# The opening of an attention block: halved loads from two queues, and a narrower first score tile

## The chip, the cores and the metric

The kernel runs on one core of one Trainium2 chip. The metric is the device time of one execution in microseconds (us), the median over several runs. The program keeps five engines busy: TensorE (PE; its weight loads are shown apart as PEld), VectorE (DVE), ScalarE (ACT), GpSimd (POOL) and SyncE (SP, which here only issues transfers). Each engine takes its instructions in order, and waits on semaphores for the others.

## What is computed

```python
q_bits = (einsum('bhsd,dk->bhsk', q, proj) > 0)
k_bits = (einsum('bhsd,dk->bhsk', k, proj) > 0)
mask = (bucket(q_bits)[..., :, None] == bucket(k_bits)[..., None, :])
scores = where(mask, q @ k.T / sqrt(64), -1e9)
x = softmax(scores) @ v            # 2 batches, 8 heads, 768 rows, 64 columns
x = gate(conv(x)) * (x @ w_val) @ w_out
u = x + real(fft2(x)); out = u + relu(norm(u) @ w_ch1) @ w_ch2
```

Queries and keys are hashed by six projections into buckets; a query attends to keys of its own bucket alone. Only the hashing and the first scores are touched here.

## The kernel before

**The stages.** `attention` walks eight pairs of heads, two heads (j = 0, 1) to a pair and six tiles of 128 query rows to a head: 96 score tiles, numbered n. Behind it come the gated projection, the Fourier mixing and a stage of channel weights. The order of the instructions is the order in which the Python code emits them (a manual schedule); nothing is reordered later.

**One score tile.** `scores(n)` multiplies a query tile by all 768 keys in two passes m (line 557). Row group m = 0 of the tiles `q2` and `k2` holds the high part of q and k, doubled; m = 1 holds in its upper half the low part of k and the high part of q, and in its first seven rows the hash bits, so that one product gives the score and pushes unequal buckets far away. `clamp(n)` on DVE (line 568) takes the minimum, `expo(n)` on ACT (line 575) the exponential, `p_transpose` turns it on PE (line 593), `p_high` on ACT and `p_low` on DVE split it, and `pv` multiplies by v (line 616). The loop over n clamps tile n+3 while it turns tile n.

**Where q and k come from.** `load(p, j)` (line 326) lets SP issue q and k of one head as one transfer each. PE turns them (64 columns of q and 64 of k beside each other, so that q lands on partitions 0 to 63 and k on 64 to 127), ACT writes the high part `ht`, DVE the low part `lt`. For the first head `start()` copies them into `q2[0]` and `k2[0]` by ACT and POOL. For the second head `qk_place(0, 1)` (lines 411 to 416) lets SP issue six transfers into `q2[1]` and `k2[1]`, and `bits_place` (line 435) two more for the bits. `scores(6)`, the first tile of the second head, waits for all eight.

**The bits of the first head.** `proj` is loaded into the tile `pr`; `project_parts(j)` splits it on POOL (lines 174, 377, 379 and 382) into `ph`, `pl` and `plus`; `project_alone` (line 448) multiplies on PE into the PSUM tile `whole`; DVE compares with zero (lines 504 and 509); for k a second step on ACT (line 505) scales the bits into `k2[0]`. The table `col` holds scale and bias by partition.

**Warm-up.** `idle(n)` (line 356) issues n matmuls of zeros: 18 ahead of the first data, three and four later.

Of the kernel before, what the change touches and what calls it, by code (L numbers as in the profile page):

```python
# [34 lines left out]
WARM = (18, 3, 4)  # L35
# [48 lines left out]
def col_table():  # L84

    c = np.zeros((P, 6), np.float32)
    c[:64, 0] = 1.0
    c[64:, 0] = KSCALE
    c[:, 2] = -1.0
    c[0, 2] = 1.0  # L90
    c[:, 3] = -8.0 * 896 * 2.0 ** 20
    c[:, 4] = -8.0 * 897 * 2.0 ** 20

    for j in (0, NR):
        c[j : j + NB, 1] = 1.0
        c[j : j + NB, 5] = -0.5
        c[j + NB, 5] = 1.0
        c[j + 32 : j + 32 + NB, 1] = -2.0 * BIG
        c[j + 32 : j + 32 + NB, 5] = BIG
        c[j + 32 + NB, 5] = 3.0 * BIG  # L100
    return c
# [3 lines left out]
def block_kernel(  # L105
# [15 lines left out]
    warm = cpool.tile([P, 1], F32, name="warm")  # L121
    nc.vector.memset(warm, 0.0)

# [178 lines left out]
    def attention(es):  # L302
# [24 lines left out]

        def load_v(p):
# [41 lines left out]
        def project_parts(j):  # L370

            for half in range(2):
# [3 lines left out]
                pool_copy(hd, pr[rs, :])  # L376
                nc.gpsimd.tensor_tensor(ld, f32(hd), pr[rs, :], op=ALU.subtract)
                pool_copy(pl[rs, j, c0 : c0 + NB], f32(hd))
                nc.gpsimd.tensor_tensor(plus[rs, j, c0 : c0 + NB], pr[rs, :], f32(hd), op=ALU.subtract)
# [12 lines left out]
        def qk_transpose(p, j, a):  # L392
# [11 lines left out]
            nc.scalar.activation(ht, tp, AF.Copy, scale=col[:, 0:1])  # L404
            nc.vector.scalar_tensor_tensor(lt, tp, col[:, 0:1], f32(ht), op0=ALU.mult, op1=ALU.subtract)
# [54 lines left out]
        def start():  # L460
# [7 lines left out]
            def turned(j, tps):  # L468
                for a in range(2):
                    for r in range(3):  # L470
                        nc.tensor.transpose(
                            tps[a][:, r * P : (r + 1) * P], rqk[:, j, 3 * a + r].rearrange("p i d -> p (i d)"), ident
                        )

            def high(j, tps):
                for a in range(2):
                    nc.scalar.activation(halves(st[0]["ht", j])[a], tps[a], AF.Copy, scale=col[:, 0:1])

            def low(j, tps):
# [950 lines left out]
```

## Time and profile before

| what | value |
| --- | --- |
| median of three runs | 617.75 us (617.74, 617.75, 620.0) |
| span of the profiled execution (first to last instruction) | 616.8 us |
| PE busy | 604.7 us, 98% |
| DVE, ACT, POOL busy | 444.7, 358.5, 269.3 us |
| first score matmul that waits for bits starts | 10.75 us into the span |
| first clamp starts | 11.40 us |

The profiled execution has no time of its own beside the three that are listed; its span is 0.95 us below their median, and that difference is taken to be what lies around the span. A busy share is an average over the stages, and the opening is 2% of the span: what it costs is read from its own rows, and what it is worth later from the stage into which it runs.

### The profile page before, as it was taken

Reading aid. Unit: us, or ns where it says so; the run is one execution under the profiler, and the core shown is the slowest. Engines: PE = TensorE matmul, PEld = TensorE weight load, DVE = VectorE, ACT = ScalarE, POOL = GpSimd, SP = SyncE. Lnnn points to the kernel's source line nnn. Section 1 sums busy time; section 2 is a strip of 40 time slices with the busy share of each in tenths; the row PEclk is TensorE's granted clock in tenths of the full one; section 3 lists DMA queues with packets and bytes.
Section 4 is the critical chain, followed back from the end, with each engine's and each line's share of the span. In section 5 each row is a group of like instructions: output and inputs, shape, how many; then the busy total and the mean of one; then the engine's idle time right before and its main releaser. Section 6 shows DMA issues by size and latency. Waiting matters only on the chain.

```text
span 616.8 us, 10435 instructions
## 1 busy us (share of the span) xinstructions
PE 604.7 (98%) x3711; PEld 537.4 (87%) x3711; DVE 444.7 (72%) x850; ACT 358.5 (58%) x712; POOL 269.3 (44%) x303
## 2 busy tenths in 40 slices
PE   7999999999999999999999999999999999999997
PEld 6889999999998889998898988888888888888886
DVE  5999999999999998898669788888885411111113
ACT  5998899998998887944625355555665111111121
POOL 8152588876888799892350633233221000000000
PEclk9999999999999999999999999999999999999999
DMA  6956686756666640262110243443440200000002
GB/s 139 210 142 164 145 178 160 164 152 156 157 154 178 171 124 14 73 231 70 36 35 0 70 133 118 125 136 108 134 135 1 103 0 1 2 0 1 0 1 102
DMA packets 54957, 62.02 MB, mean 101 GB/s; under 512 B 29184, under 2 KB 42664, under 8 KB 54650
## 3 DMA queue, kind: packets, MB, share of 16 engines
q1 hardware_dynamic: 54170, 57.81, 35.7%
q0 software_dynamic: 432, 3.55, 1.5%
q8 instruction: 29, 0.48, 0.3%
q14 instruction: 22, 0.18, 0.1%
q10 hardware_dynamic: 304, 0.01, 0.0%
HBM read 36.73 MB, written 3.19 MB: 65 GB/s over the span
## 4 chain that ended last, share of the span: by engine, by line
PE 78%; DVE 10%; DMA 4%; ACT 2%; issue 2%; SPq 2%; POOL 1%; DVEq 0%; ACTq 0%; POOLq 0%
PE pf L1337 20%; PE acc L1347 20%; PE sp L557 8%; PE op L616 7%; PE ptp L593 6%; PE ps L1154 5%; PE ps L222 3%; PE ps L1218 3%; DVE sd L568 2%; DVE ptl L605 2%; PE ps L1189 1%; DMA rqk<-in_k_dram 1%; PE late L222 1%; DMA xs<-xc 1%; PE bp L443 1%
## 5 line engine op out<-in xcount | busy, mean ns | idle before, releaser
L1347 PE MATMUL acc<-w,hid 128*128 128x512 f32 x576 | 137.4, 391 | 0.0
L1347 PEld LDWEIGHTS acc<-w,hid 128*128 128x128 f32 x576 | 105.5, 188 | 20.1
L1340 DVE SCALAR_TENSOR_TENSOR hid<-pf,hid 128x512 fp32r<-128x512 f32 (+1 forms) x62 | 33.4, 555 | 120.6 <-ACT hid L1339 120.6
L1337 PE MATMUL pf<-uth,w 128*128 128x512 f32 (+1 forms) x496 | 97.1, 337 | 0.1
L568 DVE TENSOR_SCALAR_CACHE_REDUCE sd<-sp 128x768 f32<-128x768 f32 x96 | 91.1, 950 | 7.7 <-PE sp L557 7.2
L1339 ACT ACTIVATE hid<-pf 128x512 fp32r<-128x512 f32 (+1 forms) x62 | 28.9, 488 | 115.2 <-PE pf L1337 115.2
L557 PE MATMUL sp<-qk 128*128 128x512 f32 (+1 forms) x384 | 91.5, 360 | 3.9 <-DVE sd L568 2.6
L605 DVE TENSOR_TENSOR ptl<-ptp,pth 128x768 fp32r<-128x768 f32 x96 | 91.4, 952 | 5.1 <-ACT pth L601 3.8
L1337 PEld LDWEIGHTS pf<-uth,w 128*128 128x128 f32 x496 | 79.0, 188 | 15.2 <-DVE hid L1340 1.3
L575 ACT ACTIVATE sd<-sd,nm 128x768 f32<-128x768 f32 x96 | 90.1, 939 | 1.5 <-DVE sd L568 1.5
L601 ACT CAST pth<-ptp 128x768 fp32r<-128x768 f32 x96 | 77.0, 802 | 17.7 <-PE ptp L693 8.9
L162 POOL TENSOR_TENSOR w<-cv 128x512 fp32r<-128x512 f32 x31 | 40.1, 1293 | 88.8 <-DVE cv L157 77.4
L593 PE MATMUL ptp<-ident,sd 128*128 128x128 f32 x576 | 78.6, 272 | 0.2 <-ACT sd L575 0.2
L616 PE MATMUL op<-pth,v 128*128 128x256 f32 x288 | 74.0, 283 | 1.0 <-ACT xc L629 1.0
L616 PE MATMUL op<-ptl,v 128*128 128x256 f32 x288 | 73.8, 286 | 0.0
L557 PEld LDWEIGHTS sp<-qk 128*128 128x128 f32 x384 | 58.2, 189 | 13.6 <-DVE sd L568 7.1
L593 PEld LDWEIGHTS ptp<-ident,sd 128*128 128x128 f32 x576 | 65.8, 140 | 1.1 <-ACT sd L575 0.5
L634 POOL TENSOR_TENSOR xm<-xc,xs 64x256 f32<-64x256 f32 x48 | 35.2, 734 | 59.2 <-DMA xs<-xc 38.6
L616 PEld LDWEIGHTS op<-pth,v 128*128 128x128 f32 x288 | 54.2, 188 | 5.9 <-ACT xc L629 2.0
L616 PEld LDWEIGHTS op<-ptl,v 128*128 128x128 f32 x288 | 54.3, 188 | 0.3
L1337 PE MATMUL pf<-utl,w 128*128 128x512 f32 (+1 forms) x248 | 53.1, 336 | 0.0
L149 ACT ACTIVATE cv<-cv,col 128x512 int32<-128x512 int32 x32 | 23.2, 725 | 41.5 <-DVE cv L146 41.5
(214 smaller groups left out, 998.0 us busy)
## 6 DMA issues: line engine op xcount, KB each, us to landing
raw<-in_moe_w_ch_dram SPq DMA_DIRECT2D x32, 512.0 KB
qk<-ht SPq DMA_DIRECT2D x60, 192.0 KB
qk<-lt SPq DMA_DIRECT2D x30, 192.0 KB
rqk<-in_q_dram SPq DMA_DIRECT2D x16, 192.0 KB
rqk<-in_k_dram SPq DMA_DIRECT2D x16, 192.0 KB
rv<-in_v_dram SPq DMA_DIRECT2D x8, 384.0 KB
out_dram<-o SPq DMA_DIRECT2D x12, 256.0 KB
xs<-xc SPq DMA_DIRECT2D x47, 64.0 KB
```

The costliest lines, as they stand in the source:

```text
L162: nc.gpsimd.tensor_tensor(dst()[1], fold(g.bitcast(F32)), fold(e.bitcast(F32)), op=ALU.mult)
L557: nc.tensor.matmul(sp[:, cs], q2[i][:, m, qi * P : (qi + 1) * P], k2[i][:, m, cs], start=m == order[0], stop=m == order[1])
L568: nc.vector.tensor_scalar(sd[n], sp, CLAMP, None, op0=ALU.min, op1=ALU.min, accum_out=st[p]["nm"][:, n % 12 : n % 12 + 1],)
L575: nc.scalar.activation(sd[n], sd[n], AF.Exp, bias=st[p]["nm"][:, i : i + 1], scale=-1.0, accum_out=st[p]["sums"][:, i : i + 1],)
L593: nc.tensor.transpose(tp[:, r // 3, c0 : c0 + P], sd[n][:, r * P : (r + 1) * P], ident)
L601: nc.scalar.copy(p_parts(n)[0], tp)
L605: nc.vector.tensor_tensor(lo, tp, f32(ho), op=ALU.subtract)
L616: nc.tensor.matmul(po[kb], v3[:, r, c0 : c0 + P], pt[kb][x][:, r, :], start=r == 0 and x == 0, stop=r == R - 1 and x == 1,)
L634: add[kb] = lambda: nc.gpsimd.tensor_tensor(st[p]["xm"][mr, blk * QB : (blk + 1) * QB], xc[mr, :], xs[mr, :], op=ALU.add)
L1337: nc.tensor.matmul(pf, w[:, c, :], x[:, c, cs], start=n == 0, stop=n == 3 * NC - 1)
L1340: nc.vector.scalar_tensor_tensor(hl[:, cs], pf, 0.0, f32(hh)[:, cs], op0=ALU.max, op1=ALU.subtract)
L1347: nc.tensor.matmul(acc, x[:, ts_], w, start=f == 0 and n == 0, stop=f == NF - 1 and n == 2)
```

## The change

Five things change in the first 12 us of the program.

1. `load_halves` replaces the first `load(0, 0)`: q and k of the first head come in two halves each, q issued by SP and k by ACT. `proj` follows on both queues, one half from each. 13 instead of 18 warm-up matmuls stand ahead.
2. `project_parts(0)` and the sign of `pr` run on DVE instead of POOL, ahead of the first low parts. The scale of the turned tiles comes from a constant written by DVE, no longer from `col`.
3. k's bits are written by DVE straight into `k2[0]`; q's bits are compared on DVE and then scaled on ACT, in pieces of 128, 256 and 384 columns. So the two roles are exchanged, with the columns of `col`.
4. Of q only the first 128 columns are copied ahead; the other 640 come in three POOL copies. k's first copy on POOL is split in two.
5. The second head is turned into two other PSUM banks; its two high and two low parts are spread between the first clamps and exponentials.

```diff
-WARM = (18, 3, 4)
+WARM = (13, 3, 4)
...
+        def load_halves():
+            t = st[0]["rqk"] = ap4.tile([P, 2, R, 2, D], F32, tag="rqk", name="rqk", bufs=2)
+            for a in range(2):
+                rs = slice(3 * a, 3 * a + 3)
+                for i, (eng, src) in enumerate(((nc.sync, q), (nc.scalar, k))):
+                    eng.dma_start(t[:, 0, rs, i, :], src[0, 0].rearrange("(p r) d -> p r d", r=R)[:, rs, :])
...
-        load(0, 0)
+        load_halves()
...
-        for r in (0, 64):
-            nc.scalar.dma_start(pr[r : r + 64, :], proj)
+        nc.scalar.dma_start(pr[0:64, :], proj)
+        nc.sync.dma_start(pr[64:128, :], proj)
...
-        nc.gpsimd.tensor_scalar(pr[64:128, :], pr[64:128, :], -1.0, 0.0, op0=ALU.mult, op1=ALU.add)
-        project_parts(0)
+        nc.vector.tensor_scalar(pr[64:128, :], pr[64:128, :], -1.0, None, op0=ALU.mult)
+        project_parts(0, fast=True)
...
-            high(0, first)
-            low(0, first)
-            q1, q2_ = slice(0, HS), slice(HS, S)
-            nc.scalar.copy(k2[0][0:64, 0, :], h[64:128, :])
-            pool_copy(k2[0][64:128, 0, :], h[64:128, :])
-            nc.scalar.copy(q2[0][0:64, 0, q1], h[0:64, q1])
-            nc.scalar.copy(q2[0][64:128, 1, q1], h[0:64, q1])
-            pool_copy(k2[0][64:128, 1, :], l[64:128, :])
-            pool_copy(q2[0][64:128, 0, q1], l[0:64, q1])
+            for a in range(2):
+                high(0, banks_[a], a)
+                low(0, banks_[a], a)
+                pool_copy(halves(k2_[64:128, 0, :])[a], halves(h[64:128, :])[a])
+            nc.scalar.copy(k2_[0:64, 0, :], h[64:128, :])
+            nc.scalar.copy(q2_[0:64, 0, tile0], h[0:64, tile0])
+            nc.scalar.copy(q2_[64:128, 1, tile0], h[0:64, tile0])
+            pool_copy(q2_[64:128, 0, tile0], l[0:64, tile0])
+            pool_copy(k2_[64:128, 1, :], l[64:128, :])
...
+            def k_bits(a):
                 nc.vector.tensor_scalar(
-                    halves(q2[0][0:NR, 1, :])[a], whole[qs, a, :HS], 0.0, col[qs, 5:6], op0=ALU.is_gt, op1=ALU.add
+                    halves(k2_[0:NR, 1, :])[a], whole[ks, a, :HS], 0.0, col[ks, 5:6], op0=ALU.is_gt, op1=ALU.add
                 )
...
+            def q_bits(a, cs):
+                to = slice(a * HS + cs.start, a * HS + cs.stop)
+                nc.vector.tensor_scalar(bits[qs, to], whole[qs, a, cs], 0.0, None, op0=ALU.is_gt)
+                nc.scalar.activation(
+                    q2_[0:NR, 1, to], f32(bits)[qs, to], AF.Identity, scale=col[qs, 1:2], bias=col[qs, 5:6]
+                )
+
+            k_bits(0)
+            q_bits(0, tile0)
+            k_bits(1)
+            second = two_banks()
             load_v(0)
             load(1, 0)
-            turned(1, second)
+            for a in range(2):
+                turned(1, second[a], a)
             idle(WARM[2])
-            high(1, second)
-            pool_copy(q2[0][0:64, 0, q2_], h[0:64, q2_])
...
+            sp = [scores(0, order=(0, 1))]
+            q_bits(0, slice(P, HS))
+            high(1, second[0], 0)
+            clamp(0, sp[0])
+            q_bits(1, slice(0, HS))
+            pool_copy(q2_[0:64, 0, rest], h[0:64, rest])
+            pool_copy(q2_[64:128, 0, rest], l[0:64, rest])
+            pool_copy(q2_[64:128, 1, rest], h[0:64, rest])
             project_parts(1)
-            sp = [scores(0, order=(0, 1)), scores(1, pst.tile([P, 2, 512], F32, tag="t", name="sp"))]
-            clamp(0, sp[0])
+            sp.append(scores(1, pst.tile([P, 2, 512], F32, tag="t", name="sp")))
             expo(0)
-            low(1, second)
+            low(1, second[0], 0)
+            high(1, second[1], 1)
             clamp(1, sp[1])
+            low(1, second[1], 1)
             sp = scores(2)
             values(0, 0)
             qk_place(0, 1)
```

Line numbers of the changed kernel are about 20 higher than those of before from `start()` on. Three places show how the instructions now stand.

On DVE, between the projection's split and the third clamp; first before, then in the change (`lt_170` belongs to the first head, `lt_172` to the second, `sd_250`, `sd_255`, `sd_275` are the first three clamps before, `sd_236`, `sd_259`, `sd_280` those of the change):

```order
L481 SCALAR_TENSOR_TENSOR lt_170<-bp_174,col_65,ht_169 128x384 [waits Activation_49]
L504 TENSOR_SCALAR bits_202<-bp_195 7x384 [waits PE_49]
L504 TENSOR_SCALAR bits_202<-bp_195 7x384
L509 TENSOR_SCALAR qk_152<-bp_195,col_65 7x384 [waits Pool_49]
L509 TENSOR_SCALAR qk_152<-bp_195,col_65 7x384
L568 TENSOR_SCALAR sd_250,nm_248<-sp_238 128x768 [waits PE_49]
L481 SCALAR_TENSOR_TENSOR lt_172<-tp_208,col_65,ht_171 128x384 [waits Activation_49]
L481 SCALAR_TENSOR_TENSOR lt_172<-tp_208,col_65,ht_171 128x384
L568 TENSOR_SCALAR sd_255,nm_248<-sp_243 128x768 [waits PE_49]
L568 TENSOR_SCALAR sd_275,nm_248<-sp_257 128x768 [waits PE_49]
```

```order
L488 SCALAR_TENSOR_TENSOR lt_170<-bp_174,turn_scale_68,ht_169 128x384 [waits Activation_49]
L515 TENSOR_SCALAR qk_154<-bp_196,col_65 7x384 [waits DMAHW6_49,PE_49,Pool_49]
L521 TENSOR_SCALAR bits_203<-bp_196 7x128
L515 TENSOR_SCALAR qk_154<-bp_196,col_65 7x384
L521 TENSOR_SCALAR bits_203<-bp_196 7x256
L590 TENSOR_SCALAR sd_236,nm_234<-sp_226 128x768 [waits PE_49]
L521 TENSOR_SCALAR bits_203<-bp_196 7x384
L488 SCALAR_TENSOR_TENSOR lt_172<-bp_208,turn_scale_68,ht_171 128x384 [waits Activation_49]
L590 TENSOR_SCALAR sd_259,nm_234<-sp_251 128x768 [waits PE_49]
L488 SCALAR_TENSOR_TENSOR lt_172<-bp_209,turn_scale_68,ht_171 128x384 [waits Activation_49]
L590 TENSOR_SCALAR sd_280,nm_234<-sp_262 128x768 [waits PE_49]
```

Of four comparisons of 384 columns ahead of the first clamp, two of 384, one of 128 and one of 256 are left there, and one of 384 stands behind it; the second head's low parts stand apart.

On ACT, from the last copy of the first head to the second exponential, before and in the change (`ht_171` is the second head's high part):

```order
L495 CAST qk_152<-ht_169 64x384
L505 ACTIVATE qk_154<-bits_202,col_65 7x768 [waits DVE_49,Pool_49]
L477 ACTIVATE ht_171<-tp_208,col_65 128x384 [waits PE_49]
L477 ACTIVATE ht_171<-tp_208,col_65 128x384
L575 ACTIVATE sd_250,sums_249<-sd_250,nm_248 128x768 [waits DVE_49]
L575 ACTIVATE sd_255,sums_249<-sd_255,nm_248 128x768 [waits DVE_49]
```

```order
L505 CAST qk_152<-ht_169 64x128
L522 ACTIVATE qk_152<-bits_203,col_65 7x128 [waits DMAHW6_49,DVE_49,Pool_49]
L522 ACTIVATE qk_152<-bits_203,col_65 7x256 [waits DVE_49]
L485 ACTIVATE ht_171<-bp_208,turn_scale_68 128x384 [waits PE_49]
L522 ACTIVATE qk_152<-bits_203,col_65 7x384 [waits DVE_49]
L597 ACTIVATE sd_236,sums_235<-sd_236,nm_234 128x768
L485 ACTIVATE ht_171<-bp_209,turn_scale_68 128x384 [waits PE_49]
L597 ACTIVATE sd_259,sums_235<-sd_259,nm_234 128x768 [waits DVE_49]
```

The second half of the second head's high part has moved behind q's last bits and the first exponential.

On SP, from its first transfer to the first placement of the second head, before and in the change:

```order
L326 DMA rqk_115<-in_q_dram 128x6x64
L326 DMA rqk_115<-in_k_dram 128x6x64
L326 DMA rqk_115<-in_q_dram 128x6x64
L326 DMA rqk_115<-in_k_dram 128x6x64
L331 DMA rv_209<-in_v_dram 128x2x384
L326 DMA rqk_211<-in_q_dram 128x6x64 [waits DMAHW0_49]
L326 DMA rqk_211<-in_k_dram 128x6x64 [waits DMAHW1_49]
L411 DMA qk_153<-ht_171 64x768 [waits DMAHW2_49,Activation_49]
```

```order
L335 DMA rqk_118<-in_q_dram 128x3x64 x2
L347 DMA pr_123<-in_proj_dram 64x6
L327 DMA rqk_118<-in_q_dram 128x6x64
L327 DMA rqk_118<-in_k_dram 128x6x64 [waits DMAHW0_49]
L340 DMA rv_210<-in_v_dram 128x2x384 [waits DMAHW1_49]
L327 DMA rqk_212<-in_q_dram 128x6x64 [waits DMAHW2_49]
L327 DMA rqk_212<-in_k_dram 128x6x64 [waits DMAHW3_49]
L423 DMA qk_153<-ht_171 64x768 [waits DMAHW4_49,Activation_49]
```

The second head's k now waits for the landing of the first half of k, and v and the next pair stand behind it; the first placement waits for `ht_171` in both.

## Rows read from the trace of the kernel before

**Rows 1.** The page, its first two parts: span, busy time of PE and DVE
```profile
span 616.8 us, 10435 instructions
PE 604.7 (98%) x3711; PEld 537.4 (87%) x3711; DVE 444.7 (72%) x850; ACT 358.5 (58%) x712; POOL 269.3 (44%) x303
```

**Rows 2.** Busy time by stretch: us, busy and count by engine, granted clock, DMA, GB/s
```profile
20.00:24.00 4.00, 4.00 (x32) 3.75 (x31) 4.00 (x10) 3.46 (x9) 0.00 (x0) 1.00 0.91 236
...
60.00:100.00 40.00, 39.43 (x300) 37.24 (x299) 38.43 (x73) 35.92 (x74) 27.73 (x32) 1.00 0.66 155
```

**Rows 3.** Timeline of the loading: start, duration, engine, line, operation, count, idle before
```profile
0.76 1.19 ACTq L338 DMA_DIRECT2D pr<-in_proj_dram  x2
0.76 0.69 SPq L326 DMA_DIRECT2D rqk<-in_q_dram  x1
...
2.61 1.28 ACT L341 ACT_TABLE_LOAD   x1 [2.61 <-issue]
...
4.56 0.21 POOL L382 TENSOR_SCALAR pr<-pr 64x6 f32<-64x6 f32 x1 [0.18 <-DMA pr<-in_proj_dram]
...
6.55 0.20 POOL L379 TENSOR_TENSOR plus<-pr,ph 64x6 fp32r<-64x6 f32 x1
```

**Rows 4.** Chain of waits through the opening: start, duration, what
```profile
1.50 4.12 DMA rqk<-in_k_dram
...
8.55 1.02 DVE bits L504 x2
...
9.61 1.15 DVE qk L509 x2
10.75 0.63 PE sp L557 x2
```

**Rows 5.** Timeline from the first low parts to the third clamp
```profile
6.93 1.14 DVE L481 SCALAR_TENSOR_TENSOR lt<-bp,col,ht 128x384 fp32r<-128x384 f32 x2 [5.34 <-ACT ht L477]
...
8.36 0.82 PE L471 MATMUL tp<-ident,rqk 128*128 128x128 f32 x6
...
9.67 1.03 ACT L505 ACTIVATE qk<-bits,col 7x768 fp32r<-7x768 f32 x1 [0.37 <-DVE bits L504]
...
9.82 0.62 PE L557 MATMUL sp<-qk 128*128 128x512 f32 x2 [0.17 <-POOL qk L174]
...
10.72 1.05 ACT L477 ACTIVATE ht<-tp,col 128x384 fp32r<-128x384 f32 x2
...
11.40 0.96 DVE L568 TENSOR_SCALAR_CACHE_REDUCE sd<-sp 128x768 f32<-128x768 f32 x1 [0.66 <-PE sp L557]
...
11.80 0.53 SPq L411 DMA_DIRECT2D qk<-ht  x1
...
12.40 0.94 ACT L575 ACTIVATE sd<-sd,nm 128x768 f32<-128x768 f32 x1 [0.63 <-DVE sd L568]
...
14.21 0.95 DVE L568 TENSOR_SCALAR_CACHE_REDUCE sd<-sp 128x768 f32<-128x768 f32 x1
```

**Rows 6.** Timeline around the second head's bits, its first scores and its first clamp
```profile
16.27 0.97 POOL L458 TENSOR_SCALAR bits<-bits,col 64x768 fp32r<-64x768 f32 x1 [0.71 <-ACT pth L601]
...
17.41 1.72 SPq L435 DMA_DIRECT2D qk<-bits  x2
...
21.97 0.47 PE L557 MATMUL sp<-qk 128*128 128x512 f32 x1
...
22.95 0.95 DVE L568 TENSOR_SCALAR_CACHE_REDUCE sd<-sp 128x768 f32<-128x768 f32 x1
```

**Rows 7.** Chain of waits at the next placement of bits, 34 to 38 us
```profile
35.16 2.18 DMA qk<-bits
37.34 0.25 issue
```

**Rows 8.** Instructions on the tile of the warm-up; a small DVE group (busy, mean ns)
```profile
L356 PE MATMUL idle<-zeros x25: 279/415/582, 1.7 to 9.4; 128*128 128x256 f32 x25
...
L997 DVE TENSOR_SCALAR rstd<-mu 128x6 f32<-128x6 f32 x2 | 0.2, 163 | 0.0
```

More of the change, by code (lines that the diff above doesn't have):

```diff
@@ L466, in start @@
             h, l = f32(st[0]["ht", 0]), f32(st[0]["lt", 0])
[L468 to L477, printed above, removed]
@@ L479, in low @@
-            def low(j, tps):
-                for a in range(2):
-                    nc.vector.scalar_tensor_tensor(
-                        halves(st[0]["lt", j])[a], tps[a], col[:, 0:1], f32(halves(st[0]["ht", j])[a]),
-                        op0=ALU.mult, op1=ALU.subtract,
-                    )
-            first = two_banks()
-            turned(0, first)
-            idle(WARM[1])
-            high(0, first)
-            low(0, first)
-            q1, q2_ = slice(0, HS), slice(HS, S)
-            nc.scalar.copy(k2[0][0:64, 0, :], h[64:128, :])
@@ L493, in start, with turned, high @@
-            pool_copy(k2[0][64:128, 0, :], h[64:128, :])
-            nc.scalar.copy(q2[0][0:64, 0, q1], h[0:64, q1])
-            nc.scalar.copy(q2[0][64:128, 1, q1], h[0:64, q1])
-            pool_copy(k2[0][64:128, 1, :], l[64:128, :])
-            pool_copy(q2[0][64:128, 0, q1], l[0:64, q1])
+            def turned(j, tp, a):
+                for r in range(3):
+                    nc.tensor.transpose(tp[:, r * P : (r + 1) * P], rqk[:, j, 3 * a + r].rearrange("p i d -> p (i d)"), ident)
+            def high(j, tp, a):
+                nc.scalar.activation(halves(st[0]["ht", j])[a], tp, AF.Copy, scale=turn_scale)
@@ new lines, in low @@
+            def low(j, tp, a):
+                nc.vector.scalar_tensor_tensor(
+                    halves(st[0]["lt", j])[a], tp, turn_scale, f32(halves(st[0]["ht", j])[a]),
+                    op0=ALU.mult, op1=ALU.subtract,
+                )
+            tile0, rest = slice(0, P), slice(P, S)
+            q2_, k2_ = q2[0], k2[0]
+            banks_ = two_banks()
+            for a in range(2):
+                turned(0, banks_[a], a)
+            idle(WARM[1])
+            for a in range(2):
+                high(0, banks_[a], a)
+                low(0, banks_[a], a)
+                pool_copy(halves(k2_[64:128, 0, :])[a], halves(h[64:128, :])[a])
@@ L502, in start @@
             ks, qs = slice(32, 32 + NR), slice(0, NR)
-            for a in range(2):
-                nc.vector.tensor_scalar(halves(bits)[a][ks], whole[ks, a, :HS], 0.0, None, op0=ALU.is_gt)
-            nc.scalar.activation(
-                k2[0][0:NR, 1, :], f32(bits)[ks], AF.Identity, scale=col[ks, 1:2], bias=col[ks, 5:6]
-            )
-            for a in range(2):
+            def k_bits(a):
                 nc.vector.tensor_scalar(
-                    halves(q2[0][0:NR, 1, :])[a], whole[qs, a, :HS], 0.0, col[qs, 5:6], op0=ALU.is_gt, op1=ALU.add
+                    halves(k2_[0:NR, 1, :])[a], whole[ks, a, :HS], 0.0, col[ks, 5:6], op0=ALU.is_gt, op1=ALU.add
@@ L511, in start @@
                 )
-            second = pst.tile([P, 2, 512], F32, tag="t", name="tp")
-            second = [second[:, a, :HS] for a in range(2)]
+            def q_bits(a, cs):
[3 more added lines that the diff above has]
+                    q2_[0:NR, 1, to], f32(bits)[qs, to], AF.Identity, scale=col[qs, 1:2], bias=col[qs, 5:6]
+                )
```

40 lines of the change are left out of this document (21 added, 19 removed).

## The prediction

> **What bounds the kernel now.** I read the page's first parts first [rows 1]: PE is busy for 98% of the span. A mean over stages says little of a change in the first 12 us, so the table by stretches comes next [rows 2]: between 20 and 24 us PE and DVE are both busy for 4.00 us of 4.00, and between 60 and 100 us for 39.43 and 38.43 of 40. Once the score tiles run, two engines are full. The reader is to see that a microsecond won or lost ahead of them reaches the end whole, unless a later wait takes it up. Last come the chain of waits and the timeline [rows 3, 4, 5]. The opening is one chain: k lands at 5.62 (1.50 + 4.12), the tiles are turned and split, DVE writes low parts and then bits from 8.55 to 10.76, two matmuls follow, and the first clamp starts at 11.40. From there DVE has no gap.
>
> There is a second clock beside this chain. SP places the second head by eight transfers, the first at 11.80 and the two of the bits from 17.41 [rows 5, 6]. `scores(6)` starts at 21.97 and its clamp at 22.95. I ask of every step what it does to both.
>
> **The first chain, step by step.**
>
> *Loads.* SP spends 0.69 us on issuing q [rows 3] before it can begin k at 1.50 [rows 4]. With k on ACT its issue starts 0.74 earlier, so that the last data land between 4.88 (all of it won) and 5.62 (nothing); I take 5.3, nearer to the upper row, as the bytes are the same. The Trainium skill ("DMA: Bandwidth & Descriptors", Issuing engines are not separate DMA queues) says that transfers of several issuing engines run on the same 16 DMA engines and that only the sequencer's issue time is saved; by that rule this term is at most the 0.74 of the row, and what no saving at all would make of the time is rival C. The first halves land earlier, but ACT is then still busy: four issues of about 0.6 (1.19 for two), the table load of 1.28 and a small activation end at about 4.75. So the first half gains little.
>
> *`proj` and its split.* Before, POOL got it at 4.56 and was done at 6.75 [rows 3]. Now both halves of it stand behind the halves of q and k on their queues. It lands between 4.56 and shortly after the last data, 5.9; I take 5.4, the side of the data it queues behind. DVE does nine small operations. The nearest row has 0.163 for 6 columns [rows 8]: 1.5 for nine that stand alone, and half of that, 0.7, if they overlap as neighbours on DVE do. I take 0.8, since only three of them wait for the one before. The split ends at 6.2. DVE's low parts now queue behind this wait: they run from 6.2 to 7.35 (1.14 for two [rows 5]) where before they ended at 8.07.
>
> *Projection and bits.* The bits began 0.48 after the low parts (8.55 against 8.07); so now at 7.83. Before, the four operations and the gap took 2.20 to 10.75 [rows 4]. Now three stand ahead of the first scores: 0.57, about 0.25 for 128 columns (a third of the columns and the fixed part; no less than 0.1, no more than 0.5) and 0.6: 1.4. The ACT piece of 128 columns runs beside the last of them. The last pair of score matmuls starts at 9.2, and the clamp 0.65 later as before: 9.85, against 11.40. **The opening gains 1.55.** Two things I cost at nothing, beside the bits: POOL's copy of k's low part (at most 0.97, as the other 64x768 operation [rows 6]) ends at 8.3; and PE, which needed 1.46 from the second head's transposes at 8.36 to the first pass at 9.82, 0.17 of it a wait for POOL [rows 5], gets there at 9.0 if it starts them at 7.7. Its first pass is 0.3 long; were the cover gone, that much would be lost.
>
> **What takes it back on DVE and ACT.** The second head's parts are no longer finished ahead of the first exponential. DVE clamps until 10.73, then compares q's last 384 columns (0.55) until 11.28; ACT scales them (half of 1.03 and a fixed part [rows 5], 0.55) until 11.85; only then runs `expo(0)`, 0.94, and only then the second high part, 0.58, ending at 13.4. DVE's last low part waits for it and ends at 13.95, with 0.5 of new work and some 0.7 of waiting behind it. The third clamp starts at 13.95 instead of 14.21: of 1.55 there is 0.26 left. POOL's three copies of 640 columns, 0.8 each by the same row, end at 10.7; `scores(1)` waits for them, and DVE's comparison and low part (until 11.8) cover both.
>
> **What the second clock makes of it.** `qk_place(0, 1)` needs both high parts. They ended at 11.77 (10.72 + 1.05) and SP began at 11.80; now they end at 13.4. SP then needs the same 5.61 us to the bits, which were issued at 17.41 because SP itself was free only then: POOL had finished the bits at 17.24 [rows 6]. Now POOL will be done at about 17.0 and SP arrives at 19.0. The transfers of the bits ended their issue at 19.13; the next such pair needed 2.18 us to land and 0.25 until PE started [rows 7]. 19.13 + 2.43 is 21.56, and PE started at 21.97: the slack was 0.4 at most. It may be none, as the pair queues behind 1.5 MB of placements and loads that were still moving. Delay at `scores(6)`: 1.6 less 0 to 0.4; I take 1.4, since the backlog moves with SP's start. The clamp of tile 6 then starts at 24.35 instead of 22.95, and DVE, which would have been ready at 22.7, waits.
>
> Nothing behind it has room [rows 2]: the two full engines carry 1.4 us on. The next placement of bits (PE waits for it until 37.59) hangs on the engines and moves along; for transfers that the delay lets finish ahead of their turn I take off 0.1. **Sum: the gain at the first clamp does not survive, and the kernel ends 1.3 us later.** Against the execution profiled that is a span of 618.1 instead of 616.8; its 0.95 around the span kept, the median goes from 617.75 to **619.1 us**, +0.2%. A measurement of this kernel can tell about 0.5%, 3.1 us, from no change; so I forecast no change that can be told.
>
> **The rivals.**
>
> *A, the placement is covered.* If `scores(6)` has more slack than the next pair's rows suggest, or a later wait takes the stall up, the 0.26 at the third clamp stays, and up to 0.9 if `proj` lands by 4.7: 617.75 - 0.4 = 617.3. For it: the trace books no wait of `scores(6)` on a transfer. Against it: PE had only just ended its transposes, and no engine had a gap. It decides where the placement may slip by more than 1.6 us. Chance 0.2.
>
> *B, TensorE's clock rises late.* 25 matmuls of zeros took 279 to 582 ns with a median of 415 [rows 8]: most ran at 1.2 GHz, the last ones at 2.4 GHz. The page grants the full clock in every stretch it records, so the rise lies inside the warm-up. Now 13 stand there instead of 18 and end at about 4.4, and only six transposes and three idle matmuls run until the split is done at 6.2. If the clock is still at 1.2 GHz at the projection, the critical matmuls (one of 384 columns, two of the first scores, 0.63 together with their drain) take up to twice as long: 0.5 at the clamp, and as much at the placement, up to 0.9 with the transposes. Result 619.1 + 0.9 = 620.0: slower than before by 2.2. The point: whether the level is 2.4 GHz when the first projection starts. The Trainium skill ("TensorE: Matmul & The Clock Gate", What's actually happening) says that the number of slow matmuls at a kernel's start differs from run to run; by that rule this could strike some executions alone, and no run here shows it yet. Chance 0.1.
>
> *C, the loads win nothing.* Same bytes, same DMA engines, and `proj` last: the data land at 5.6, `proj` at 6.2, the split ends at 7.0 and everything above shifts by 0.8: clamp at 10.65, placement at 14.2, tile 6 later by 2.2: 619.9. This is also the case in which the change does not do what its halves are for. For it: 24-byte rows of `proj` behind 256-byte rows of q on both queues. Chance 0.1.
>
> **How the numbers follow.** My forecast, 618.4 to 619.8, has 0.55; A 0.2, B 0.1, C 0.1; 0.05 is left for what I have not seen. One of the three runs before lies at 620.0, so a median can sit high without any mechanism. The range reaches from A's (617.3 less its 0.5) to B and C together (620.5): 616.8 to 620.5. Faster by over 0.5% (below 614.7) would need a gain of 3.1 us, twice what the first chain gives: 0.02. Slower by over 0.5% (above 620.8) needs B and C at once, or a longer stall: 0.06. Within: 0.92.
>
> **What would show it.** Right: the first clamp at 9.4 to 10.4; DVE idle by 0.4 to 0.9 us ahead of the second low part of the second head, released by ACT; SP's first placement at 13.0 to 13.9; PE, and behind it DVE, idle for over a microsecond at tile 6, released by a transfer of the bits, with its clamp at 24 to 25. Wrong: a placement that starts before 12.3, or a clamp of tile 6 at or before 22.95; the step to blame is then the order on ACT or the slack. A first clamp behind 10.8 points to B (matmuls of zeros still near 415 ns) or C (DVE waiting for `pr` beyond 6 us).

## The result, and the profile after

The change makes the kernel slower: **625.29 us** (median of six executions, 623.74 to 629.47) against 617.87 us (617.0 to 620.0) on the same chip, a ratio of **1.0118** with a 95% interval of 1.0086 to 1.0150. The forecast was 619.1 us with a range up to 620.5; 1.3 us was expected, 7.4 came. The execution profiled took 629.47 us, the longest of the six: TensorE's clock fell twice in it, as will be seen (mean granted clock 0.994; the two shortest executions, 623.74 and 624.04 us, have 0.999).

The page after, first parts; the busy times answer to [rows 1]:

```profile
span 627.7 us, 10434 instructions
PE 608.7 (97%) x3706; PEld 542.0 (86%) x3706; DVE 446.5 (71%) x862; ACT 358.8 (57%) x714; POOL 268.3 (43%) x295
```

The span is 10.9 us longer; PE is busy for 4.0 of it, DVE for 1.8. So PE both waits more and works more slowly.

The opening as predicted: the chain of waits after (start, duration, what), beside [rows 3, 4].

```profile
1.86 3.27 DMA pr<-in_proj_dram
...
5.23 0.17 DVE ph L388
...
6.20 0.07 DVE plus L391
6.27 0.03 issue
6.30 0.63 DVE lt L488
...
9.17 1.10 PE sp L579 x4
10.26 0.02 issue
10.29 0.97 DVE sd L590 x2
```

And the timeline after (start, duration, engine, line, operation, tiles; idle time before in brackets), beside [rows 5]:

```profile
4.87 0.17 DVE L394 TENSOR_SCALAR pr<-pr 64x6 f32<-64x6 f32 x1 [3.06 <-DMA pr<-in_proj_dram]
...
11.17 0.54 DVE L521 TENSOR_SCALAR bits<-bp 7x384 fp32r<-7x384 f32 x1
...
12.36 0.92 ACT L597 ACTIVATE sd<-sd,nm 128x768 f32<-128x768 f32 x1
...
13.28 0.56 ACT L485 ACTIVATE ht<-bp,turn_scale 128x384 fp32r<-128x384 f32 x1
...
13.86 0.53 SPq L423 DMA_DIRECT2D qk<-ht  x1
...
13.87 0.62 DVE L488 SCALAR_TENSOR_TENSOR lt<-bp,turn_scale,ht 128x384 fp32r<-128x384 f32 x1 [0.64 <-ACT ht L485]
14.40 0.95 DVE L590 TENSOR_SCALAR_CACHE_REDUCE sd<-sp 128x768 f32<-128x768 f32 x1
```

The first clamp starts 1.11 us earlier (10.29 for 11.40). The first exponential does not: 12.36 for 12.40. SP's first placement is 2.06 late (13.86 for 11.80), and the third clamp 0.19 late. Then the second clock, beside [rows 6, 7]; first the timeline, then the chain of waits:

```profile
16.46 0.97 POOL L470 TENSOR_SCALAR bits<-bits,col 64x768 fp32r<-64x768 f32 x1 [1.43 <-ACT sd L597]
...
19.47 1.73 SPq L447 DMA_DIRECT2D qk<-bits  x2
...
24.97 1.01 PE L579 MATMUL sp<-qk 128*128 128x512 f32 x4 [2.72 <-DMA qk<-bits]
25.79 0.42 PE L638 MATMUL op<-pth,v 128*128 128x256 f32 x1
...
26.02 0.96 DVE L590 TENSOR_SCALAR_CACHE_REDUCE sd<-sp 128x768 f32<-128x768 f32 x1 [0.84 <-PE sp L579]
```

```profile
20.43 4.30 DMA qk<-bits
24.73 0.25 issue
24.97 1.01 PE sp L579 x4
```

POOL has the bits ready at 17.4, SP comes to them at 19.47, the second of their transfers lands 4.30 after its issue began, and PE stands still for 2.72. By stretches, beside [rows 2] (us, busy and count of PE, PEld, DVE, ACT, POOL, granted clock, DMA share, GB/s):

```profile
20.00:24.00 4.00, 2.25 (x18) 1.92 (x17) 3.08 (x6) 3.45 (x7) 0.00 (x0) 1.00 0.98 187
24.00:28.00 4.00, 3.03 (x15) 2.97 (x16) 2.05 (x4) 0.43 (x3) 0.00 (x0) 0.71 1.09 261
28.00:32.00 4.00, 4.00 (x28) 3.85 (x27) 2.68 (x5) 3.46 (x7) 0.73 (x1) 0.86 0.83 190
```

Behind the stall the granted clock goes down: a matmul of 256 columns takes 0.42 at 25.79, and from 29.74 on 0.28 again. The Trainium skill ("TensorE: Matmul & The Clock Gate", What's actually happening) says that the clock knows two levels only and that idleness brings the lower one; the mean of 0.71 is then a mixture of 1.2 and 2.4 GHz, and the stretch from 26 to 28 us alone is indeed granted 0.50.

The prediction has no word on the next two places. First, near 255 us, where attention hands over to the gated projection (of after, then of before; timeline):

```profile
260.45 1.03 PE L223 MATMUL late<-x,wvh 128*128 128x384 f32 x4 [2.07 <-DVE g L232]
```

```profile
252.68 0.86 PE L222 MATMUL late<-x,wvh 128*128 128x384 f32 x4
```

The first matmul into `late` waits 2.07 for DVE's gate in the change and for nothing before. Second, the last stages. Page, costliest groups (count, busy us, mean ns, idle before), after and before:

```profile
L1359 PE MATMUL pf<-uth,w 128*128 128x512 f32 (+1 forms) x496 | 97.6, 339 | 0.1
...
L1359 PE MATMUL pf<-utl,w 128*128 128x512 f32 (+1 forms) x248 | 53.8, 338 | 0.0
```

```profile
L1337 PE MATMUL pf<-uth,w 128*128 128x512 f32 (+1 forms) x496 | 97.1, 337 | 0.1
...
L1337 PE MATMUL pf<-utl,w 128*128 128x512 f32 (+1 forms) x248 | 53.1, 336 | 0.0
```

The same 744 matmuls, no edit near them, and 1.2 us more. DVE adds their results up in `hid`; the 33rd and the last of its 62 such writes (timeline, before and then after) lie 116.89 us apart before and 117.80 after:

```profile
488.42 0.69 DVE L1340 SCALAR_TENSOR_TENSOR hid<-pf,hid 128x512 fp32r<-128x512 f32 x1 [2.67 <-ACT hid L1339]
...
605.31 0.42 DVE L1340 SCALAR_TENSOR_TENSOR hid<-pf,hid 128x256 fp32r<-128x256 f32 x1 [0.47 <-ACT hid L1339]
```

```profile
498.09 0.69 DVE L1362 SCALAR_TENSOR_TENSOR hid<-pf,hid 128x512 fp32r<-128x512 f32 x1 [2.68 <-ACT hid L1361]
...
615.89 0.42 DVE L1362 SCALAR_TENSOR_TENSOR hid<-pf,hid 128x256 fp32r<-128x256 f32 x1 [0.52 <-ACT hid L1361]
```

### The profile page after: what moved, and what is told of

It is laid out like the page before. It is cut to its first block, busy times and chain, and to the rows that moved or that the text cites. A ratio compares the mean times of both kernels' runs of the same rounds, so it can differ in the third digit from the quotient of the medians.

```text
span 627.7 us, 10434 instructions
## 1 busy us (share of the span) xinstructions
PE 608.7 (97%) x3706; PEld 542.0 (86%) x3706; DVE 446.5 (71%) x862; ACT 358.8 (57%) x714; POOL 268.3 (43%) x295
## 4 chain that ended last, share of the span: by engine, by line
PE 71%; DVE 14%; DMA 5%; ACT 4%; issue 2%; SPq 2%; POOL 1%; ACTq 0%; POOLq 0%; DVEq 0%
PE pf L1359 20%; PE acc L1369 19%; PE sp L579 6%; PE ps L1176 5%; PE op L638 5%; PE ptp L615 4%; DVE ptl L627 4%; DVE sd L590 4%; PE ps L223 3%; PE ps L1240 3%; DMA qk<-ht 2%; PE late L223 2%; PE ps L1211 1%; ACT sd L597 1%; DMA xs<-xc 1%
## 5 line engine op out<-in xcount | busy, mean ns | idle before, releaser
L242 POOL TENSOR_TENSOR g<-g,conv_tmp 128x768 f32<-128x768 f32 x27 | 46.4, 1719 | 1.2
```

The source lines that it names most:

```text
L242: nc.gpsimd.tensor_tensor(dst, dst, tmp, op=ALU.add)
```

## The experiments

Four suspects came out of the two traces: the late placement, the clock behind the stall, the PSUM banks at 255 us, and SBUF addresses in the last stages. `start()` takes its turned tiles from a pool of two banks (tag "t"). Before, it takes three tiles (`whole`, `tp`, `sp`), now two, since the second head goes into other banks. From there on all turned tiles stand in the other bank of the two, and so does the last `early` tile of attention: bank 4 before, now bank 2, which the first `late` tile takes next. And the new tile `turn_scale` fills a slot of 32 bytes, so that all tiles behind it lie 32 bytes higher. (The trace names neither banks nor addresses: both are worked out from how the program places its tiles, and e1 and e4 test the one, e5 and e6 the other.)

The table shows where each run's profile stands against the kernel before: differences of start, in us, of the clamp of tile 40 (before: 105.62), that of tile 92 (230.28), the first `late` matmul (252.68), the 33rd and the last of DVE's 62 writes of `hid` from `pf` (488.42 and 605.31), and the span.

| run | clamp 40 | clamp 92 | late | hid 33 | hid 62 | span |
| --- | --- | --- | --- | --- | --- | --- |
| the change | +4.50 | +5.54 | +7.77 | +9.67 | +10.58 | +10.9 |
| e12, the change again | +2.09 | +2.83 | +5.06 | +6.97 | +7.88 | +8.2 |
| e1, banks back | +2.33 | +3.98 | +3.98 | +4.20 | +5.11 | +5.4 |
| e2, high part early | +0.27 | +1.81 | +4.05 | +5.97 | +6.88 | +7.2 |
| e3, both | -0.20 | +0.58 | +0.58 | +0.80 | +1.71 | +2.0 |
| e4, before, banks turned | +1.22 | +0.09 | +2.35 | +4.00 | +4.00 | +4.0 |
| e5, both and addresses | +0.04 | +0.86 | +0.86 | +0.95 | +0.95 | +1.3 |
| e6, before, 32 bytes more | +0.72 | -0.41 | -0.43 | -0.19 | +0.72 | +0.7 |
| e7, before, high part late | +2.60 | +4.49 | +4.47 | +4.49 | +4.49 | +4.5 |
| e8, other order | +0.58 | +0.94 | +3.16 | +3.34 | +3.34 | +3.6 |
| e9, other order again | +0.37 | -0.09 | -0.09 | -0.07 | -0.07 | +0.2 |
| e10, change, PE kept busy | +2.54 | +0.87 | +3.10 | +3.41 | +4.32 | +4.6 |
| e11, e5 with whole loads | +0.37 | -0.48 | -0.48 | -0.26 | -0.26 | -0.2 |

Read the columns as steps. Between tile 40 and tile 92 every run drifts by up to 2 us, in both directions, kernels of the old opening too (e6 -1.1, e7 +1.9). The waits for transfers differ there: near 195 us ACT waits 2.12 for a placement into `qk` in the change, where it waited 1.00 before. Nothing shows this drift to be a part of the change. The other steps follow the edits.

**e1: the banks turned back.** The changed kernel with one more tile of the pool, written by two matmuls of zeros.

```diff
             sp = scores(2)
+            skip = pst.tile([P, 2, 512], F32, tag="t", name="skip")
+            st[0]["skip"] = skip[:, 0, : 2 * P]
+            nc.tensor.matmul(st[0]["skip"], zeros[:, 0:P], zeros, start=True, stop=True)
...
                 tile_, tp = p_transpose(n)
+                if n == 0:
+                    nc.tensor.matmul(st[0]["skip"], zeros[:, 0:P], zeros, start=True, stop=True)
```

> The changed kernel with two extra matmuls of zeros (0.12 us each) into a bank of the turned tiles, one behind the third scores and one behind the first turn, so that the two banks alternate again as before the change and the last early tile stands in bank 4 instead of 2. Theory (two places: the late placement of the second head, and the banks): the wait of the late matmuls near 253 us and the clock fall behind it are gone, the stall at tile 6 stays; 625.3 less 2.2 to 3.9, so 621.4 to 623.1. Rival 1 (the opening alone makes the whole loss, what happens later follows from it): no change, 625. Rival 2 (the new order of the transfers' semaphores makes the later stalls): no change, 625.

Measured 621.97 us (620.82 to 625.76), ratio 1.0059 (1.0036 to 1.0082). The step at `late` is gone: +3.98 on both sides of it, against +5.54 to +7.77 in the change. The stall of the opening is still there, without a fall of the clock (timeline, then stretches):

```profile
24.39 0.94 PE L582 MATMUL sp<-qk 128*128 128x512 f32 x4 [1.75 <-DMA qk<-bits]
```

```profile
24.00:28.00 4.00, 3.62 (x27) 3.47 (x28) 2.81 (x6) 2.32 (x7) 0.00 (x0) 1.00 0.87 222
```

**e2: the high part in its old place.** The changed kernel with the second half of the second head's high part directly behind the first half.

```diff
             high(1, second[0], 0)
+            high(1, second[1], 1)
             clamp(0, sp[0])
...
             low(1, second[0], 0)
-            high(1, second[1], 1)
             clamp(1, sp[1])
```

> The changed kernel with the second half of the second head's high part moved on ACT from behind the first exponential to directly behind its first half. Theory: SP's first placement starts at 11.5 to 11.8 instead of 13.86, scores of tile 6 at 21.7 to 22.3 instead of 24.97, PE does not idle long enough there for its clock to fall; the wait near 253 us stays. 625.3 less 3.0 to 4.7: 620.6 to 622.3. Rival 1 (the opening alone makes the whole loss): 617 to 618. Rival 2 (the load by halves and its stragglers make the bits late): scores of tile 6 stay at 24 or later, 624 to 625.

Measured 623.01 us (620.87 to 625.77), ratio 1.0062 (1.0041 to 1.0083). That is above the 620.6 to 622.3 expected. The place was right, but the change loses 2.3 us there and not the 3.0 to 4.7 expected. SP's first placement is at 11.83, scores(6) at 22.14 without a wait, and at tile 40 only 0.27 is left. This one line makes the stall (timeline):

```profile
11.83 0.53 SPq L423 DMA_DIRECT2D qk<-ht  x1
...
22.14 0.94 PE L579 MATMUL sp<-qk 128*128 128x512 f32 x4
```

**e3: both.**

> Both edits in one kernel: high part ahead of the first exponential, banks alternating as before. Theory: nothing of the loss is left and what the opening wins at the third clamp (about 0.5) may stay if the bits land in time; 617.0 to 618.2. Rival (a third cause, such as the order of the semaphores of the transfers, makes part of the loss): 619 or more.

Measured 620.50 us (618.91 to 623.24), ratio 1.0029 (1.0003 to 1.0054). The theory, that nothing is left, missed; the rival, a third cause, holds (619 or more). At tile 40 the kernel is 0.20 ahead of the one before. Of what is left, 0.8 is the drift up to tile 92, 0.2 comes between `late` and `hid` 33, and 0.91 in the last stages, between the two `hid` columns.

**e4: the banks alone.** The two matmuls of e1 in the kernel before, which puts its `early` tile into bank 2.

> The kernel before with the same two matmuls of zeros, which here turn the alternation of the two banks over, so that the last early tile stands in bank 2, where the first late tile goes. Nothing else of the change. Theory: the late matmuls near 253 us wait for DVE's gates as they do in the changed kernel, 2.1 us, and PE's clock may fall behind it, 1.7 us more; up to 0.7 us in the opening, where the first turn now waits for another clamp. 617.9 plus 2.2 to 4.5: 620.1 to 622.4. Rival (the wait near 253 us is a follow-up of the opening): 617.9 to 618.6.

Measured 622.81 us (621.78 to 625.85), ratio 1.0065 (1.0045 to 1.0085), 0.4 above the expected range. The old opening with the banks turned has the step, and the fall of the clock behind it:

```profile
255.03 0.96 PE L222 MATMUL late<-x,wvh 128*128 128x384 f32 x4 [2.09 <-DVE g L231]
```

```profile
256.00:260.00 4.00, 4.00 (x16) 4.00 (x16) 2.60 (x6) 3.39 (x8) 3.92 (x5) 0.57 0.02 4
```

It gives +2.26 from tile 92 to `late` and 1.65 more by `hid` 33. (The 1.22 at tile 40 come from this run's opening, where the first clamp was 0.41 late and `scores(6)` 1.19; by tile 92 they are given back.)

**e5: addresses as before.** e3, with `turn_scale` in the second word of `warm`'s slot.

```diff
-    warm = cpool.tile([P, 1], F32, name="warm")
-    turn_scale = cpool.tile([P, 1], F32, name="turn_scale")
+    pair = cpool.tile([P, 2], F32, name="pair")
+    warm, turn_scale = pair[:, 0:1], pair[:, 1:2]
```

> The version with both repairs (banks turned back, second high part of the second head right behind the first), and with the scale of the turned tiles kept in the second word of the tile `warm` instead of a tile of its own, so that every later SBUF tile lies where it lies before the change (32 bytes lower). Theory (addresses): the drift of 1.1 to 1.4 us between 485 us and the end goes; the group pf of the last stages returns from 339 to 337 ns, the span is within 0.7 us of the one before, the ratio 1.000 (0.998 to 1.002), about 618.5 us. Rival (the drift comes from something else that the change moved): the drift stays, ratio 1.002 to 1.003, as in the run with both repairs.

Measured 618.80 us (617.72 to 621.87) against 618.96 of before in the same batch, ratio 1.0001 (0.9980 to 1.0022). The drift is gone: +0.95 at both `hid` columns, and the group on the page is back at 337:

```profile
L1364 PE MATMUL pf<-uth,w 128*128 128x512 f32 (+1 forms) x496 | 97.0, 337 | 0.1
```

**e6: addresses alone.** The kernel before with one written tile of four bytes.

```diff
     warm = cpool.tile([P, 1], F32, name="warm")
+    spare = cpool.tile([P, 1], F32, name="spare")
     nc.vector.memset(warm, 0.0)
+    nc.vector.memset(spare, 0.0)
```

> The kernel before with one written tile of four bytes per partition more behind `warm`, and nothing else: all later SBUF tiles lie 32 bytes higher. Theory (addresses): no difference up to about 485 us, then 1.1 to 1.4 us more to the end, pf at 339 ns instead of 337; ratio 1.002, about 619.2 us. Rival: a 4-byte constant costs nothing, ratio 1.000, pf at 337 ns.

Measured 619.52 us (618.25 to 620.89), ratio 1.0005 (0.9986 to 1.0024): too little for the medians, but plain in the profile, where `hid` goes from -0.19 to +0.72 and

```profile
L1339 PE MATMUL pf<-uth,w 128*128 128x512 f32 (+1 forms) x496 | 97.6, 339 | 0.0
```

In all fourteen profiles the time from the 33rd to the last `hid` is 116.89 us where the tiles lie as before (seven profiles) and 117.80 where they lie 32 bytes higher (seven).

**e7: the late high part in the kernel before.**

```diff
-            high(1, second)
+            high(1, second, (0,))
...
             expo(0)
+            high(1, second, (1,))
             low(1, second)
```

> The kernel before with one move: the second half of the second head's high part stands behind the first exponential on ACT. Theory (the late placement alone makes the stall): SP's first placement starts at 13.7 to 14.0 instead of 11.80, scores(6) at 23.7 to 25.0 instead of 21.97, its clamp by 1.7 to 3 later, and this reaches the end whole; with a fall of TensorE's clock behind the stall 1.5 more. No step at 253 us and no drift. 619.6 to 622.4 us, ratio 1.003 to 1.007. Rival (the placement has slack, the stall of the change comes from the other loads): scores(6) within 0.5 of 21.97; only DVE's wait for the low part counts, 618.0 to 619.0 us, ratio 1.000 to 1.002.

Measured 621.89 us (620.21 to 623.14), ratio 1.0044 (1.0024 to 1.0063). The size is as the first theory said, the way is not. Here both low parts stand ahead of the second clamp, so DVE itself waits 1.56 for ACT, the second clamp comes 1.95 late (the first was 0.30 late already), and scores(6) at 24.41 waits 0.41 for DVE and not for the bits. So e7 shows that the late half costs some 2.3 by tile 40 (2.60 less the 0.30); that the bits are the carrier is shown by e1 and e2 and not by it.

**e8 and e9: can the gain be kept?** In e3 the first clamp starts at 10.33, 1.07 early, and the first low part of a turned tile at 17.12, as before. The first exponential waits on ACT behind q's last 384 columns. e8 puts both high parts first and those columns behind the exponential:

```diff
-            q_bits(0, slice(P, HS))
             high(1, second[0], 0)
+            high(1, second[1], 1)
+            q_bits(0, slice(P, HS))
             clamp(0, sp[0])
-            q_bits(1, slice(0, HS))
...
             expo(0)
             low(1, second[0], 0)
-            high(1, second[1], 1)
-            clamp(1, sp[1])
             low(1, second[1], 1)
+            clamp(1, sp[1])
+            q_bits(1, slice(0, HS))
```

> The changed kernel with banks and addresses as before, and another order: both high parts of the second head stand on ACT ahead of q's later bits, the bits of q's last 384 columns behind the first exponential (compared on DVE behind the second clamp). Theory (the gain of the opening was lost to ACT's order): SP's first placement at 10.4 to 10.9, the first exponential at 11.2 to 11.6 instead of 12.40, DVE's bits of the second head at 14.5 to 14.8 instead of 15.09, scores(6) at 21.4 to 21.7 instead of 21.97, and this reaches the end: 0.3 to 0.6 us below the kernel before, ratio 0.999. Rival (the placement of the bits ends when it ends, as the transfers ahead of it set it): scores(6) at 21.8 to 22.1 and ratio 1.000. Third: the order costs more on PE or POOL than it wins, scores(6) above 22.3, ratio above 1.001.

Measured 623.10 us (621.57 to 625.73), ratio 1.0071 (1.0044 to 1.0097). The first exponential is early (11.68), but the second waits 1.47 behind q's columns, which wait for a comparison behind the second clamp: scores(6) at 22.61. The third of the expected outcomes came, the order that costs more than it wins. And the step at `late` is back (+2.22). The likely reason, which no run tests by itself: the pool hands out the bank whose last reader comes first in the program, and as `whole` is now read later, `skip` went into the other bank and turned nothing. If that is so, e8 is a second test of the banks, if not a planned one.

e9 puts `q_bits(1, ...)` directly behind `expo(0)`:

> As the run with both high parts first, but q's last 384 columns are compared on DVE ahead of the second head's low parts and scaled on ACT directly behind the first exponential; banks and addresses as before the change. Theory (DVE carries the gain once no engine stands in the way): first exponential at 11.3 to 11.7, third clamp near 13.9, DVE's bits of the second head at 14.6 to 14.9 instead of 15.09, scores(6) at 21.4 to 21.8 instead of 21.97; 0.2 to 0.5 us below the kernel before at tile 8, no step at 253 us, no drift; ratio 0.999 to 1.000. Rival: another wait takes it, tile 8 within 0.1 of before or later, ratio 1.000 to 1.002.

Measured 618.57 us (617.27 to 622.40) against 617.98, ratio 1.0015 (0.9998 to 1.0032). The rival holds. The first clamp starts at 10.21 and the first exponential at 11.21, but the transposes of tile 0 go into the bank of `scores(1)` and wait for its clamp:

```profile
13.82 0.85 PE L618 MATMUL ptp<-ident,sd 128*128 128x128 f32 x6 [1.00 <-DVE sd L593]
```

They begin at 13.82, in the kernel before at 13.57. None of the versions tried beats the kernel before.

**e10: PE busy in the gap.** The changed kernel with 20 idle matmuls ahead of scores(6).

```diff
+            if n == 3:
+                to = pss.tile([P, 2, 512], F32, tag="s", name="idle")
+                for _ in range(20):
+                    nc.tensor.matmul(to[:, 0, : 2 * P], q2[0][:, 0, 0:P], k2[0][:, 0, 0 : 2 * P], start=True, stop=True)
             if n + 3 < NT:
```

> The changed kernel with 20 idle matmuls of 256 columns (products of tiles that are there, into the score tile's bank ahead of its use) on PE ahead of scores(6), and nothing else: PE has work in the gap of 2.7 us, the bits land when they land. Theory (the fall of TensorE's clock behind the stall costs 1.5 us of its own): scores(6) still at 24.5 to 25.1, the granted clock stays 1.00 between 24 and 32 us, tile 8 is 2.6 to 3.2 us later than before the change instead of 4.5; the step of 2.2 at 253 us, with a fall behind it, stays. Rival (the gap does not set the clock): the clock falls all the same and tile 8 is 4.5 later.

Measured 623.45 us (623.21 to 625.87), ratio 1.0093 (1.0079 to 1.0107). As the theory has it, scores(6) starts at 24.56 and the clock stays at 1.00:

```profile
24.00:28.00 4.00, 3.94 (x30) 3.56 (x29) 2.61 (x6) 1.72 (x4) 0.00 (x0) 1.00 0.87 211
```

Tile 40 is 2.54 late and not 4.50. But near 255 us PE waits 2.10 as ever, and this time no fall follows, so one profile does not prove that the 20 matmuls kept the clock up. e12, without them, has no fall behind this stall either.

**e11: whole loads.** e5 with q and k of the first head loaded whole by SP.

```diff
-        load_halves()
+        load(0, 0)
```

> The version with both repairs and the addresses as before, with q and k of the first head loaded whole by SP as before the change; proj still one half on each queue. Theory (the halves win at the first clamp and nothing at the end): the last data land 0.7 to 1.1 later than 4.62, the first clamp at 10.7 to 11.2 instead of 10.33, the first exponential at 12.4 to 13.0, scores(6) within 0.4 of 21.81, and the end within 0.5 us of the version with halves: ratio 1.000 to 1.001. Rival (the opening passes on what the loads win): first clamp, scores(6) and the end all later by 0.5 to 1, ratio 1.001 to 1.002.

Measured 618.47 us (617.71 to 623.17) against 617.98, ratio 1.0016 (1.0001 to 1.0031); e5 had 1.0001 (0.9980 to 1.0022), and the intervals overlap. Chain of waits:

```profile
1.50 3.63 DMA rqk<-in_k_dram
...
10.85 0.97 DVE sd L593 x2
```

The halves from two queues are worth 0.54 at the first clamp (10.85 against 10.31 in e5), 0.33 at tile 40, and nothing that can be told at the end, where this run's span is the shorter one (616.6 against 618.1). `scores(6)` came at 22.36, outside the 0.4 around 21.81 that was expected, and 1.0016 lies in the rival's range, so the medians leave the rival open. The Trainium skill ("DMA: Bandwidth & Descriptors", Issuing engines are not separate DMA queues) allows such a split no more than the sequencer's issue time, 0.74 by [rows 3, 4]; the 0.54 does not exceed it. But the 0.54 need not be all that the landing won: in e5 PE comes to the first transposes straight from its warm-up and does not wait for data (chain of waits):

```profile
1.72 3.14 PE idle L365 x13
4.86 1.28 PE bp L482 x6
```

**e12: the change again.**

> The changed kernel itself, unaltered, for a second profile. Theory: scores(6) between 23.5 and 25.0 with its release by a transfer of the bits, a wait for DVE of 2.0 to 2.3 us ahead of the first late matmul near 255 us, last stages with the longer matmul spacing; a fall of the clock behind either stall may be there or not, and where it is not the span is shorter by 1.5 to 1.7 for each. Ratio 1.009 to 1.013. Rival (the profile seen first was an exception): scores(6) by 22.5 and no step at 253 us.

Measured 624.13 us (623.65 to 626.76) against 617.98, ratio 1.0110 (1.0094 to 1.0127). PE waits 1.89 at scores(6), no fall follows; it waits 2.08 at `late`, and a fall does:

```profile
24.16 0.94 PE L579 MATMUL sp<-qk 128*128 128x512 f32 x4 [1.89 <-DMA wvr<-in_moe_w_val_dram]
```

```profile
256.00:260.00 4.00, 2.26 (x9) 2.26 (x10) 3.02 (x6) 3.92 (x10) 3.20 (x3) 0.80 0.00 0
260.00:264.00 4.00, 4.00 (x20) 4.00 (x19) 2.47 (x5) 2.11 (x5) 4.00 (x5) 0.77 0.00 0
```

The profile names the transfer issued two places behind the bits as the releaser, not one of the bits, against the expectation's word; scores(6) is where it said. 2.19 us late at 24.16, 3.00 late in the first profile: the 4.30 for the bits' landing there was on the long side.

## Why the prediction was wrong

**The direction and the mechanism were right, and stood for a third of the loss.** The gain at the first clamp does not survive, SP's first placement is late, `scores(6)` starves, and nothing behind takes it up: the offset at tile 12 is that at tile 60 to within 0.02 in both profiles of the change. The signs that were to show it came: first clamp at 10.29 (9.4 to 10.4 was said), DVE's wait 0.64 (0.4 to 0.9), placement at 13.86 (13.0 to 13.9, just), PE idle for 2.72 at tile 6. Only that tile's clamp, said to come at 24 to 25, came at 26.02, and at 25.14 in e12.

**First step that failed: the split of `proj`.** "I take 0.8, since only three of them wait for the one before." It took 1.40, from 4.87 to 6.27: the nine operations are 0.15 to 0.17 long, some start 0.07 to 0.08 behind the one before, others 0.17 to 0.20, and 0.19 is a second wait for `pr`. `proj` landed half a microsecond earlier than taken, and the two errors cancel: the split ended at 6.27 for 6.2. The terms behind it were each short by 0.06 to 0.15 (DVE's three comparisons took 1.55, from 7.98 to 9.53, where 1.4 stood). So the gain at the first clamp is 1.11 and not 1.55, and all that follows is 0.45 later: third clamp 14.40 for 13.95, placement 13.86 for 13.4.

**Second: the slack of the bits.** "The slack was 0.4 at most", and 1.4 was taken for a delay of 1.6. SP came 2.06 late to its placements and `scores(6)` was 2.19 to 3.00 late (e12 and the first profile). The runs show no slack. The landing of 2.18 us from [rows 7] was the wrong row, and it was added in the wrong place: its 35.16 is where the issue of the second transfer began, and the sum added the 2.18 to an issue's end, 19.13. Counted as the row counts, from 18.36, PE could have started at 20.79, and the slack would have been 1.2. The bits took longer: behind loads and placements the landing took 4.30 in the first profile and some 3.3 in e1 (second issue at 20.81, PE at 24.39 less the 0.25). Right price: 2.1 to 2.6 at tile 40 without a fall of the clock (e12, e1, e10), where 1.3 stood.

**Third: a stall has a price behind itself.** Rival B looked for the clock at the start. In the two profiles of the change it did no harm there; in e1, with the same opening, the first projection's matmuls took 0.52 instead of 0.39 and the first clamp came at 10.67 instead of 10.29 (timeline, the change and then e1):

```profile
6.09 0.39 PE L460 MATMUL bp<-ht,ph 128*64 128x384 f32 x1
```

```profile
6.58 0.52 PE L460 MATMUL bp<-ht,ph 128*64 128x384 f32 x1
```

So B's mechanism exists, with 0.4 where 0.5 stood, and it is not what made the loss. The clock fell behind the stalls: in the first profile the delay grew from 3.07 at the clamp of tile 6 to 4.50 at tile 40; behind `late`, e4 lost 1.65 between `late` and `hid` 33. It does not fall each time. Executions of the change with a mean granted clock of 0.999 or 1.000 took 623.65 to 624.13, one with 0.998 took 624.64, and those with 0.994 to 0.996 took 625.94 to 629.47.

**Fourth, the largest: two edits were not costed at all.** The change's own heading said "other banks", the text asked of every step what it does to two clocks in the opening, and to nothing later. One tile fewer from a pool of two banks turns the alternation for all 96 tiles, and 240 us later a wait appears that was absent only because the banks happened to differ: 2.2 us, and 1.7 more where the clock falls (e1, e2, e4, e8). And one constant of four bytes moves every tile behind it: 0.9 in the last 117 us (e3, e5, e6), up to 1.2 over both groups of `pf`.

**The sum that the runs give**: 2.3 for the late placement, 2.2 for the banks, 0.9 to 1.2 for the addresses, 5.4 to 5.7 in all. With it go one or two falls of the clock of some 1.5 to 1.7 in part of the executions, and the waits between tile 40 and tile 92, 0.7 and 1.0 in the two profiles of the change; that makes the medians of +6.2 (e12) and +7.4. Undoing the three gives the time of before (e5, 1.0001).

**Rival A** (the placement is covered) falls with e2 against the change. **Rival C** (the loads win nothing) is refuted at the first clamp, where e11 shows 0.54; at the end no gain can be told. The range's upper end, B and C at once, was put at 620.5, where their 0.9 and 0.8 added to 619.1 make 620.8; the measured time lies beyond both.

**Open:** what decides whether the clock falls behind a stall of two microseconds; the wait at `late` was 2.06 to 2.10 in e2, e4, e8, e10 and e12, and a fall followed in e2, e4 and e12 only. The mean granted clocks of all executions say how often: the kernels with that wait (the change, e2, e4, e8, e10) have 0.997 or less in 24 of 43, the other variants in 12 of 74, and the kernel before in 2 of the 78 that ran beside the experiments. So a fall goes with that wait more often, and comes without it too. In e4 the eight executions with 0.997 (621.78 to 625.85) are no longer than the two without (622.09 and 622.99): there the 1.65 of the profile is lost in the spread. Why 32 bytes change the pace of these matmuls was not tried further either: all later tiles move together in e6, so it isn't known which operand counts.

## What to carry to other kernels

Ask of an edit not only what it does where it stands, but which shared sequences it shifts: the turn of a pool's banks and the addresses of all later tiles change with one tile more or fewer, and their price can lie hundreds of microseconds away, in code that no line of the diff touches. Look in the order of the new program for waits that changed their engine far from the edit, and keep tile counts and slots as they were (a spare word of an old tile costs nothing). A stall of the engine that bounds the kernel is to be priced with what its clock may do afterwards.

## What the hardware showed that was not expected

The granted clock fell to half behind stalls of PE of 2.07 to 2.72 us, in the first profile near 26 us and 261 us, and by the profiles this cost about 1.5 to 1.7 us each time; with the same program it stayed at 1.00 behind a stall of 1.89 (e12), and in e10 behind one of 2.10. And the same stretch of matmuls took 116.89 us, or 117.80 where all later tiles lie 32 bytes higher, alike within 0.003 us in every profile of a kind.
